# A one-core kernel of two-level attention and a gated feed-forward: when the coarse rows are loaded, where two group sums stand, which queue loads the last v rows, and how the coarse pieces are dealt out to chunks

## The chip, the cores and the metric

The program runs on one core of one Trainium2 chip. The metric is the device time of one execution in microseconds (us); the median of three runs of the kernel before is 1115.64 us (1114.74 to 1118.12). TensorE (PE) multiplies and transposes, VectorE (DVE) and ScalarE (ACT) do the elementwise work, GpSimd (POOL) some of it, and SyncE (SP) only starts transfers. ACT and POOL start transfers too. Every engine works its own list in order: an instruction that waits holds up all that stand behind it on the same engine.

## The reference

Inputs are q, k, v of 8 batches, 8 heads, 576 positions and 64 columns, and three weights of a gated feed-forward.

```python
q_d = q.reshape(B, H, Sd, factor, D).mean(axis=3)      # factor 4; k_d, v_d alike
out_d = sm_attn(q_d, k_d, v_d)
out_up = np.repeat(out_d, factor, axis=2)
mask = np.abs(pos[:, None] - pos[None, :]) < factor
out_local = softmax(where(mask, scale * q @ k^T, -1e9)) @ v
x = (out_up + out_local), heads side by side            # 4608 tokens x 512
xn = x / sqrt(mean(x * x) + 1e-6) * rms_g
out = (silu(xn @ w_gate) * (xn @ w_val)) @ w_out         # 512 -> 1536 -> 512
```

## The kernel before

**Chunks.** The 4608 tokens are worked in 18 chunks of 256 (NCH, numbered from 0). Of each chunk the feed-forward (class Forward) runs over 12 slices f of 128 hidden columns: `first` (L1327) is 24 matmuls for gate and value, then come tanh on ACT (L1335), gate and product on DVE (L1338, L1343), a split of the result in two parts (L1349 on ACT, L1352 on DVE or POOL) and, two slices later, `second` (L1363), 6 matmuls into the output. Each product is made of three matmuls, since numbers are kept as a high and a low part.

**Coarse attention.** It is cut into 32 coarse pieces, one for each batch and pair of heads, numbered 0 to 31 (class Coarse): a score (L524), a softmax, a swap (transposes, L564), values (L579), and a store of the result `o_g` to a tensor `up` in DRAM (L596), one such tensor for each pair of batches. A piece needs the sums over groups of four positions of q, k and v: class Sums, one object for each batch and half of its heads, so that two pieces share one. Its tiles qk and vs are loaded by SP (L358, L362), and three more loads each, which add to what is there, are started by POOL (L366); each of the three must wait until the one before has landed. Each tile name has two buffers.

**Rows of the coarse result.** A chunk's attention needs its rows of `up`. Class Attention loads them into `up_t` in `load_up` (four transfers of a chunk, L783), class Dense in its own `load_up` (L1189). All of these are started by ACT.

**The first three chunks** get their local attention as full scores under a mask (class Dense): the values step (L1166) reads v rows that `load_rows` (L1028) and, for the last row of chunk 0, `load_edge` (L1039) put into the four kv buffers. From chunk 3 on the local attention is elementwise on DVE, ACT and POOL (class Attention: L701, L705, L748, L755, L774), with its own k, v and q loads into the same kv buffers (L607).

**Two ways in which the order is set.** The opening (coarse pieces 0 to 7, attention of chunks 0 and 1, the decoding of 36 weight pieces, the feed-forward of chunk 0) is a list: class Plan takes tasks with an engine, a cost, a due time and buffers, plays them through, and writes the instructions in that order. A weight piece is decoded by `last_bits` on POOL (L267), a scaling on ACT (L257), a join on DVE (L274), a high part on ACT (L286, L284) and a low part (L298 on DVE; for w_out L296 on DVE or L294 on POOL, as the plan chooses). Four of the late pieces pass one after another through a single buffer named `raw`. What is written after the list is ordered by the framework's scheduler, which may also put an instruction without a due time far ahead, into gaps of the list. `tc.issue_after(x)` forbids that it stands ahead of x. PE's instructions after the list are tied to each other in this way.

**Chunks 1 on.** While chunk c runs, the attention of chunk c + 1 is made, and coarse pieces are worked at the slices that PIECES names: score at slice f, swap at f + 2, values at f + 3. All of pieces 8 to 15 (the second pair of batches) must be stored before the second half of chunk 4 can load its rows. Group sums are written at slices 0 and 6 of every chunk, or when a piece first asks for them.

Line numbers in prose are those of the profile of this kernel.

## Time and profile before

| what | value |
|---|---|
| median of three runs | 1115.64 us |
| the profiled execution | 1120.63 us |
| its span, first to last instruction | 1118.4 us |
| PE busy, DVE busy, ACT busy, POOL busy | 94%, 79%, 54%, 19% of the span |
| start of the first matmul of the feed-forward, chunks 0, 1, 2, 3, 4, 5 | 94.8, 161.3, 230.0, 300.7, 366.1, 419.6 us |
| chunk to chunk from chunk 5 on | 55.5 us, from chunk 12 on (no coarse pieces left) 50.8 us |

The profile is of one execution. PE is busy nearly all of the span, so what can be won is where it isn't: the time before 94.8 us, the chunks 0 to 3, which take 65 to 71 us in place of 55.5, and nothing after. The clock column of a stretch is the TensorE clock that was granted, as a share of 2.4 GHz; 0.5 is the lower of its two levels.

### The profile page before, as it was taken

How to read it: one execution, taken by the hardware profiler on the slowest of the kernel's cores; microseconds unless marked ns; L12 is line 12 of the kernel's file. 1: busy time of each engine (PE TensorE's matmuls, PEld its weight loads, DVE VectorE, ACT ScalarE, POOL GpSimd, SP SyncE). 2: the span in 40 equal slices, each digit the busy share in tenths (PEclk: the TensorE clock that was granted, in tenths of full speed). 3: DMA queues.
4: the chain of work that ended last, by engine and by line, in shares of the span. 5: the costliest groups of instructions: out<-in, count | busy, mean ns of one | idle time of the engine just before them, and what ended most of it. 6: DMA issues, size and time to landing. Idle time of an engine off the chain costs nothing.

```text
span 1118.4 us, 23630 instructions
## 1 busy us (share of the span) xinstructions
PE 1054.7 (94%) x8804; PEld 964.9 (86%) x8804; DVE 888.9 (79%) x1850; ACT 603.2 (54%) x2182; POOL 210.4 (19%) x269
## 2 busy tenths in 40 slices
PE   4886887999998999999999999999999999999998
PEld 3565776889897999999999999999999999999997
DVE  5867962987696989797989797979798989987422
ACT  5556732384454656565655555555647383737222
POOL 2244650032311121212121203010102020101000
PEclk9877998999998999999999999999999999999999
DMA  8676363456453343434354444313131322310000
GB/s 260 197 237 228 132 143 67 107 127 138 93 131 68 108 99 108 99 111 96 111 96 121 89 122 90 106 43 99 47 97 53 102 62 76 88 42 20 1 20 19
DMA packets 72681, 113.26 MB, mean 101 GB/s; under 512 B 25974, under 2 KB 33910, under 8 KB 72566
## 3 DMA queue, kind: packets, MB, share of 16 engines
q1 hardware_dynamic: 46422, 91.66, 27.2%
q0 software_dynamic: 8640, 15.93, 9.3%
q10 hardware_dynamic: 17504, 4.16, 1.7%
q8 instruction: 69, 1.13, 0.4%
q14 instruction: 46, 0.38, 0.1%
HBM read 99.92 MB, written 11.80 MB: 100 GB/s over the span
## 4 chain that ended last, share of the span: by engine, by line
PE 79%; DVE 7%; DMA 6%; ACT 4%; issue 3%; POOL 0%; ACTq 0%; SPq 0%; DVEq 0%; POOLq 0%
PE ps_h L1327 46%; PE ps_o L1363 23%; DMA qk<-in_qk_sum_dram 3%; PE ps_a L579 2%; ACT prod L748 2%; PE ps_a L524 1%; DVE prod L701 1%; PE ps_a L850 1%; PE ps_a L564 1%; DMA wv<-in_qk_sum_dram 1%; ACT a_g L555 1%; DMA up<-o_g 1%; PE ps_a L1143 1%; DMA q_t<-in_q_band_dram 1%; DVE sc L705 1%
## 5 line engine op out<-in xcount | busy, mean ns | idle before, releaser
L1363 PE MATMUL ps_o<-wo,hs 128*128 128x512 f32 x1296 | 339.2, 400 | 5.1 <-DVE hs L1352 3.3
L1327 PE MATMUL ps_h<-xh,wg 128*128 128x256 f32 x1728 | 317.6, 280 | 0.0
L1327 PE MATMUL ps_h<-xh,wv 128*128 128x256 f32 x1728 | 312.0, 277 | 0.0
L1327 PEld LDWEIGHTS ps_h<-xh,wg 128*128 128x128 f32 x1728 | 266.8, 190 | 8.1 <-issue 2.7
L1363 PEld LDWEIGHTS ps_o<-wo,hs 128*128 128x128 f32 x1296 | 231.2, 190 | 46.1 <-DVE hs L1352 4.1
L1327 PEld LDWEIGHTS ps_h<-xh,wv 128*128 128x128 f32 x1728 | 264.4, 188 | 2.8 <-issue 0.4
L748 ACT ACTIVATE prod<-kv,sc 128x64 f32<-128x64 f32 x960 | 246.5, 407 | 24.7 <-DMA up<-o_g 10.3
L1327 PE MATMUL ps_h<-xl,wg 128*128 128x256 f32 x864 | 244.4, 283 | 6.2 <-DVE sil L1343 3.8
L1327 PE MATMUL ps_h<-xl,wv 128*128 128x256 f32 x864 | 240.3, 278 | 4.4 <-DVE sil L1338 4.4
L1335 ACT ACTIVATE sil<-ps_h 128x256 f32<-128x256 f32 x216 | 81.7, 379 | 223.5 <-PE ps_h L1327 212.2
L1327 PEld LDWEIGHTS ps_h<-xl,wg 128*128 128x128 f32 x864 | 163.5, 189 | 14.3 <-DVE sil L1343 5.7
L1327 PEld LDWEIGHTS ps_h<-xl,wv 128*128 128x128 f32 x864 | 162.9, 189 | 7.5 <-DVE sil L1338 6.0
L1349 ACT ACTIVATE hs<-sil 128x256 fp32r<-128x256 f32 x216 | 89.4, 414 | 145.1 <-DVE sil L1343 119.5
L755 POOL TENSOR_TENSOR prod<-sc,kv 128x256 f32<-128x256 f32 x120 | 90.3, 790 | 407.0 <-DVE sc L739 202.7
L774 DVE TENSOR_REDUCE x_t<-prod 128x128 f32<-128x896 f32 x120 | 127.9, 1076 | 34.2 <-PE ps_a L850 26.3
L1338 DVE SCALAR_TENSOR_TENSOR sil<-sil,ps_h 128x256 f32<-128x256 f32 x216 | 89.0, 413 | 70.9 <-ACT sil L1335 67.0
L701 DVE TENSOR_TENSOR prod<-q_t,kv 128x896 f32<-128x896 f32 x120 | 129.6, 1082 | 5.4 <-DMA kv<-in_k_pad_dram 4.6
L705 DVE TENSOR_REDUCE sc<-prod 128x14 f32<-128x896 f32 x120 | 128.8, 1074 | 0.0
L1352 DVE TENSOR_TENSOR hs<-sil,hs 128x256 fp32r<-128x256 f32 x208 | 98.7, 476 | 32.6 <-ACT hs L1349 32.4
L1343 DVE SCALAR_TENSOR_TENSOR sil<-sil,ps_h 128x256 f32<-128x256 f32 x216 | 89.7, 416 | 2.8 <-PE ps_h L1327 1.3
L366 POOL DMA_DIRECT2D qk<-in_qk_sum_dram x36 | 32.7, 909 | 237.7 <-DMA qk<-in_qk_sum_dram 163.2
L755 DVE TENSOR_TENSOR prod<-sc,kv 128x128 f32<-128x128 f32 x120 | 51.4, 453 | 0.8
(182 smaller groups left out, 943.9 us busy)
## 6 DMA issues: line engine op xcount, KB each, us to landing
kv<-in_k_pad_dram SPq DMA_DIRECT2D x60, 320.0 KB
kv<-in_v_pad_dram SPq DMA_DIRECT2D x60, 320.0 KB
qk<-in_qk_sum_dram POOLq DMA_DIRECT2D x36, 288.0 KB, 4.9
q_t<-in_q_band_dram SPq DMA_DIRECT2D x60, 128.0 KB
out_dram<-o_sb SPq DMA_DIRECT2D x30, 256.0 KB
vs<-in_v_sum_dram POOLq DMA_DIRECT2D x36, 144.0 KB, 3.4
qk<-in_qk_sum_dram SPq DMA_DIRECT2D x12, 288.0 KB
wo<-in_qk_sum_dram SPq DMA_DIRECT2D x2, 1152.0 KB
```

What stands on the lines that cost most here:

```text
L701: nc.vector.tensor_tensor(out=pr, in0=bcast(q[:, s0:s0 + 2], 2, NO), in1=window(k, s0), op=ALU.mult)
L705: nc.vector.tensor_reduce(out=self.sc[:, j, par, s0:s0 + 2], in_=self.pr[i], axis=AX.X, op=ALU.add,)
L748: nc.scalar.activation(out=self.pr[i][:, o, s], in_=self.v[j, par][:, s0 + s + o], func=AF.Copy, scale=p[:, s, o:o + 1],)
L755: (nc.vector if engine == "DVE" else nc.gpsimd).tensor_tensor(out=self.pr[i][:, a:b], in0=bcast(p[:, :, a:b].rearrange("p s o -> p o s"), ...
L774: nc.vector.tensor_reduce(out=self.x[j][:, s0:s0 + 2, par], in_=pr.rearrange("p o s d -> p s d o"), axis=AX.X, op=ALU.add,)
L1327: last = nc.tensor.matmul(out=self.p[f][:, t], lhsT=wi(f)[:, 0, k], rhs=xi[:, k], start=(n == 0), stop=(n == 3 * KT - 1),).ins
L1335: nc.scalar.activation(out=self.sil[f], in_=self.p[f][:, 0], func=AF.Tanh, scale=0.5)
L1338: nc.vector.scalar_tensor_tensor(out=self.sil[f], in0=self.sil[f], scalar=1.0, in1=self.p[f][:, 0], op0=ALU.add, op1=ALU.mult,)
L1343: nc.vector.scalar_tensor_tensor(out=self.sil[f], in0=self.sil[f], scalar=0.5, in1=self.p[f][:, 1], op0=ALU.mult, op1=ALU.mult,)
L1349: nc.scalar.activation(out=self.hs[f][:, 0], in_=self.sil[f], func=AF.Copy)
L1352: (nc.gpsimd if engine == "POOL" else nc.vector).tensor_tensor(out=self.hs[f][:, 1], in0=self.sil[f], in1=self.hs[f][:, 0], op=ALU.subtract,)
L1363: last = nc.tensor.matmul(out=self.o[j], lhsT=lhs[:, cols], rhs=rhs(f)[:, 0], start=(f == 0 and i == 0), stop=(f == NF - 1 and i == 2),).ins
```

## The change

It has four parts and a fifth that goes with them.

1. `load_up` of Attention and of Dense (after the list) may not be issued ahead of the last copy of chunk 0's output, the list's end (`listed`, `behind`).
2. The two group sums of batch 2 are planned as tasks of the list, due 95 and 103; the two of batch 3 are written at slices 6 and 11 of chunk 1.
3. `load_edge` is started by POOL in place of SP.
4. PIECES: chunk 1 takes four coarse pieces (slices 0, 5, 7, 8), chunk 2 two (0, 3). Chunk 3 keeps two.
5. The v rows of chunk 0 are due earlier (`V_ROWS - 14`, which was `- 9`), so SP starts them ahead of the first weights.

```diff
-PIECES = {1: (0, 5, 8), 2: (0, 3, 6), 3: (0, 2)}
+PIECES = {1: (0, 5, 7, 8), 2: (0, 3), 3: (0, 2)}
+SUMS = {(1, 6): (3, 0), (1, 11): (3, 2)}
...
+    def behind(ins):
+        return tc.issue_after(ins) if ins else nullcontext()
...
-            for t in range(2):
-                nc.scalar.dma_start(out=up[:, t], in_=src[:, :, t, ui])
+            with behind(listed[-1]):
+                for t in range(2):
+                    nc.scalar.dma_start(out=up[:, t], in_=src[:, :, t, ui])
...
-                    t = task("SP", 0.7, lambda a=a: self.load_edge(b, a), V_ROWS - 4.0, [t], uses=[v], dma=0.3)
+                    t = task("POOL", 1.0, lambda a=a: self.load_edge(b, a), 0.0, [t], uses=[v], lag=2.5)
...
-                    V_ROWS - 9.0 + 2 * b + 0.1 * a if at is None else at + 2 * b + a, after, allocs=[v], uses=[v], dma=0.262 * MB,
+                    V_ROWS - 14.0 + 1.0 * b + 0.1 * a if at is None else at + 2 * b + a, after, allocs=[v], uses=[v], dma=0.262 * MB,
...
+            with behind(listed and listed[-1]):
+                for g in range(2):
...
+    for half in range(2):
+        sums[2, half] = Sums(2, half, 125.0 + 8 * half)
...
+    listed.append(opened.copied)
...
-            if f in (0, 6):
+            if (c, f) in SUMS:
+                sums_of(*SUMS[c, f])
+            if f in (0, 6) and c > FIRST:
```

What moves is seen best in the engines' lists. In the changed kernel line numbers are higher by 1 to 7 (L783 is L789, L1207 is L1214, L366 is L367, L267 is L268, L524 is L529, L1327 is L1334, L1363 is L1370).

On ACT, near the end of the opening, where the squares of chunk 0 (L1207) are followed by the weights' scaling. First before, then after:

```order
L286 ACTIVATE wg_0_688<-o_sb,g_sb 128x4x128
L1207 ACTIVATE x_t,ss<-ps_o 128x256
L783 DMA up_t<-up 128x1x64 x3
L1207 ACTIVATE x_t,ss<-ps_o 128x256 x3
L286 ACTIVATE wv_0_754<-o_sb,g_sb 128x4x128
L257 ACTIVATE o_sb<-wg_1_637 128x512
```

```order
L258 ACTIVATE o_sb<-wg_1_624 128x512
L1214 ACTIVATE x_t,ss<-ps_o 128x256 x4
L287 ACTIVATE wg_0_779<-o_sb,g_sb 128x4x128
L258 ACTIVATE o_sb<-wg_1_643 128x512 x2
L258 ACTIVATE o_sb<-wv_1_688 128x512
```

Chunk 3's four loads of coarse rows, which the scheduler had put between the squares, are gone from here; they now stand just after the copies of chunk 0's output.

On POOL, from the last weights to the end of the list. Before, all twelve adding loads of batch 2 stand behind the last weight piece:

```order
L267 TENSOR_SCALAR raw<-raw 128x512
L294 TENSOR_TENSOR wo_1_1734<-o_sb,wo_1_1733 128x512
L1352 TENSOR_TENSOR hs<-sil,hs 128x256 x2
L267 TENSOR_SCALAR raw<-raw 128x512
L366 DMA qk<-in_qk_sum_dram 128x576
L366 DMA vs<-in_v_sum_dram 72x512
L366 DMA qk<-in_qk_sum_dram 128x576
L366 DMA vs<-in_v_sum_dram 72x512
L366 DMA qk<-in_qk_sum_dram 128x576
L1352 TENSOR_TENSOR hs<-sil,hs 128x256
```

After, they stand between the weights, the first of them behind the 28th of the 36 pieces; this is the middle of that stretch:

```order
L367 DMA qk<-in_qk_sum_dram 128x576
L268 TENSOR_SCALAR raw<-raw 128x512
L367 DMA vs<-in_v_sum_dram 72x512
L1359 TENSOR_TENSOR hs<-sil,hs 128x256 x2
L268 TENSOR_SCALAR wo_1_489<-wo_1_489 128x512
L268 TENSOR_SCALAR wo_1_1242<-wo_1_1242 128x512
L367 DMA qk<-in_qk_sum_dram 128x576
L367 DMA vs<-in_v_sum_dram 72x512
L268 TENSOR_SCALAR wo_2_830<-wo_2_830 128x512
L268 TENSOR_SCALAR wo_2_918<-wo_2_918 128x512
L367 DMA qk<-in_qk_sum_dram 128x576
L268 TENSOR_SCALAR raw<-raw 128x512
```

The adding loads no longer end the list; weight pieces that pass through `raw` now stand behind them. POOL does two low parts (L294) and two splits (L1352) fewer in the list, DVE two more of each (L296, L1352); one sum of v (L441) goes from POOL to DVE far ahead of this.

On PE, at the start of chunk 1, the score of piece 8. Before, it stands ahead of the fourth slice; after, ahead of the second (slices are 24 matmuls of L1327 or L1334):

```order
L1327 MATMUL ps_h<-xl,wg_0_688 128x256
L1327 MATMUL ps_h<-xh,wg_0_688 128x256
L1327 MATMUL ps_h<-xh,wg_0_689 128x256
L524 MATMUL ps_a<-qk 72x144 x4
L1143 MATMUL ps_a<-ident_sb,prod 64x64 x16
```

```order
L1370 MATMUL ps_o<-wo_2_1866,hs 128x512 x2
L1370 MATMUL ps_o<-wo_2_1867,hs 128x512
L1334 MATMUL ps_h<-xh,wv_0_845 128x256
L1334 MATMUL ps_h<-xh,wv_0_846 128x256
L529 MATMUL ps_a<-qk 72x144 x4
L1334 MATMUL ps_h<-xl,wg_0_779 128x256
```

The score asks for its sums about two slices earlier; the transposes of chunk 2's scores (L1143, now L1149) follow one slice later.

## Rows read from the trace of the kernel before

**Rows 1.** Windows: us, busy of PE, PEld, DVE, ACT, POOL; clock, DMA share, GB/s.
```profile
161.00:230.00 69.00, 58.11 (x589) 52.88 (x588) 39.29 (x86) 23.97 (x86) 9.01 (x11) 0.93 0.44 96
230.00:300.00 70.00, 68.91 (x544) 62.09 (x544) 54.37 (x124) 39.27 (x153) 17.10 (x21) 1.00 0.58 123
475.00:531.00 56.00, 56.00 (x439) 52.01 (x438) 50.00 (x106) 33.45 (x132) 11.43 (x15) 1.00 0.43 104
```
**Rows 2.** Timeline of ACT near the opening's end: start, us, what, [idle before <-releaser].
```profile
85.06 1.90 ACTq L783 DMA_DIRECT2D up_t<-up  x3
87.01 0.38 ACT L1207 ACTIVATE x_t<-ps_o 128x256 f32<-128x256 f32 x1 [6.20 <-issue]
```
**Rows 3.** Timeline of PE at the same place.
```profile
81.20 0.43 PE L1178 MATMUL ps_o<-o_g,q_t 72*32 72x128 f32 x8
...
91.44 1.94 PE L1249 MATMUL ps_h<-ident_sb,x_t 128*128 128x128 f32 x8 [8.79 <-DVE x_t L1237]
```
**Rows 4.** Timeline of DVE: same place, then two operations of the list's end.
```profile
88.25 0.16 DVE L1216 TENSOR_TENSOR rms<-ss 128x2 f32<-128x2 f32 x1 [3.83 <-ACT x_t L1207]
...
148.25 0.68 DVE L296 TENSOR_TENSOR wo<-o_sb,wo 128x512 fp32r<-128x512 f32 x1
...
157.65 0.41 DVE L1352 TENSOR_TENSOR hs<-sil,hs 128x256 fp32r<-128x256 f32 x1
```
**Rows 5.** The window of 94 to 150 us, columns as in the first group.
```profile
94.00:150.00 56.00, 48.11 (x313) 43.08 (x314) 51.62 (x82) 36.47 (x76) 30.93 (x30) 0.94 0.47 160
```
**Rows 6.** Chain that ended last, at chunk 1's start: start us, us, what.
```profile
154.33 7.03 DMA qk<-in_qk_sum_dram
...
161.70 4.99 DMA qk<-in_qk_sum_dram
...
167.09 9.36 DMA qk<-in_qk_sum_dram
```
**Rows 7.** Timeline of PE in chunk 1's first slices.
```profile
176.59 1.24 PE L524 MATMUL ps_a<-qk 64*72 64x144 f32 x8 [7.26 <-DMA qk<-in_qk_sum_dram]
177.75 1.97 PE L1143 MATMUL ps_a<-ident_sb,prod 128*64 128x64 f32 x32
...
180.04 0.63 PE L1327 MATMUL ps_h<-xh,wg 128*128 128x256 f32 x2
...
183.14 0.39 PE L1327 MATMUL ps_h<-xh,wg 128*128 128x256 f32 x2
...
184.03 1.15 PE L1143 MATMUL ps_a<-ident_sb,prod 128*64 128x64 f32 x32
```
**Rows 8.** The window of 170 to 180 us, columns as in the first group.
```profile
170.00:180.00 10.00, 3.41 (x41) 2.96 (x42) 1.32 (x4) 0.87 (x5) 0.00 (x0) 0.60 0.43 94
```
**Rows 9.** Timeline of POOL: an early gap, and its last split of chunk 0.
```profile
51.05 1.30 POOL L267 TENSOR_SCALAR wg<-wg 128x512 uint32<-128x512 uint16 x1 [10.89 <-DMA wg<-in_w_gate_dram]
...
158.08 0.90 POOL L366 DMA_DIRECT2D qk<-in_qk_sum_dram  x1 [1.33 <-DMA qk<-in_qk_sum_dram]
158.65 1.08 POOL L1352 TENSOR_TENSOR hs<-sil,hs 128x256 fp32r<-128x256 f32 x1
```
**Rows 10.** Timeline of PE: who waits for that split.
```profile
159.79 1.66 PE L1363 MATMUL ps_o<-wo,hs 128*128 128x512 f32 x6 [1.74 <-POOL hs L1352]
```
**Rows 11.** DMA issues of 100 to 180 us: count, KB each, median us to landing.
```profile
qk<-in_qk_sum_dram POOLq DMA_DIRECT2D x6, 288.0 KB, 6.3
```
**Rows 12.** Timeline of SP: the four edge loads, a fetch into the buffer raw, its next.
```profile
47.81 2.31 SPq L1039 DMA_DIRECT2D kv<-in_v_sum_dram  x4
...
116.18 0.33 SPq L253 DMA_DIRECT2D raw<-in_w_gate_dram  x1
...
128.62 0.33 SPq L253 DMA_DIRECT2D raw<-in_w_val_dram  x1
```
**Rows 13.** Chain that ended last, end of chunk 3.
```profile
337.17 6.12 DMA up<-o_g
```
**Rows 14.** Timeline of ACT at that place.
```profile
344.65 0.38 ACT L1335 ACTIVATE sil<-ps_h 128x256 f32<-128x256 f32 x1 [4.84 <-PE ps_h L1327]
```

More of the change, by code (lines that the diff above doesn't have):

```diff
@@ L443, in add_v @@
             )
-    loose = []
+    loose, listed = [], []
+    def behind(ins):
+        return tc.issue_after(ins) if ins else nullcontext()
     used = {"wg": [], "wv": [], "wo": []}
@@ L1038, in load_edge @@
             at = v_sum.offset + ((b * FAC * HALF + HALF - 1) * 2 + a) * DM
-            nc.sync.dma_start(
+            nc.gpsimd.dma_start(
                 out=t[:, :, 1],
@@ L1187, in load_up @@
             src = up_dram[0].rearrange("b k t (s g) d -> s g (b k t) d", g=UPP)[:, self.u0:self.u0 + 2]
-            for g in range(2):
-                nc.scalar.dma_start(out=self.up[g * 16:(g + 1) * 16].rearrange("p (h d) -> p h d", d=D), in_=src[:, g])
+            with behind(listed and listed[-1]):
+                for g in range(2):
+                    nc.scalar.dma_start(out=self.up[g * 16:(g + 1) * 16].rearrange("p (h d) -> p h d", d=D), in_=src[:, g])
         def add_rows(self):
@@ L1370, in copy @@
             self.o_sb[j] = ffn.tile([P, DM], FP32, name="o_sb", bufs=W_BUFS)
-            nc.scalar.copy(out=self.o_sb[j], in_=self.o[j])
+            self.copied = nc.scalar.copy(out=self.o_sb[j], in_=self.o[j]).ins
         def store(self, j):
@@ L1487, in attn_moe_kernel @@
         decode(n)
+    for half in range(2):
+        sums[2, half] = Sums(2, half, 125.0 + 8 * half)
     for c in range(FIRST):
-        Forward(atts[c]).plan(
+        opened = Forward(atts[c])
+        opened.plan(
             first_weights if c == 0 else lambda f: [],
@@ L1497, in attn_moe_kernel @@
     loose.append(True)
-    def behind(ins):
-        return tc.issue_after(ins) if ins else nullcontext()
+    listed.append(opened.copied)
     att, late = atts[FIRST], []
```

## The prediction

> **What bounds the kernel now.** I read first the windows of a chunk each. From chunk 5 on PE is busy without a gap and a chunk takes 55.5 us (the window from 475 us) [rows 1]; there nothing can be won by moving loads. Chunk 1 takes 68.7 us with 58.1 of 69 us busy at a mean clock of 0.93, chunk 2 70.7 us with PE busy 68.9 of 70 [rows 1]: it works off what chunk 1 left behind. So PE is the bound from 230 us on, and a microsecond that PE gets back ahead of 230 us is one off the end, unless something else becomes late. Then I looked in the timelines for what PE waits for before that. Two places stand out.
>
> The first is the end of the opening. ACT has done one of the four squares of chunk 0, then stands 6.20 us in three transfers that load coarse rows [rows 2]: they wait for the store of piece 7. The squares, the root on DVE and PE's transposes all come behind that, and PE idles 8.79 us [rows 3].
>
> The second is chunk 1's first score. Its sums are not ready: three rounds of adding loads follow each other in the chain, 7.03, 4.99 and 9.36 us [rows 6], and PE waits 7.26 us for the last [rows 7], with the clock falling to a mean of 0.60 in that stretch [rows 8].
>
> **Part 1, coarse rows behind the list's end.** Removed: the four transfers between the squares. The tensor that the other three squares read was finished when PE's last add ended, 81.20 + 0.43 = 81.63 us [rows 3]; they began at 87.01 [rows 2]. So x of chunk 0 is ready 5.3 us earlier. The transposes, 1.94 us at 91.44 [rows 3], come behind an idle PE; with a shorter gap they may save another 0.9 (at the higher level the 32 smaller ones of rows 7 took 1.15 us where they took 1.97 behind a gap, so about half is lost): 6.2 at most. But chunk 0's feed-forward then waits for its weights: DVE is busy 51.6 of the 56 us up to 150 us [rows 5], decoding. What DVE gets back is the 3.83 us that it stood idle for those squares [rows 4], and that is my value, **-3.8**; the ends are 0 (weights set the pace throughout) and -6.2. Added: the transfers in chunk 1 or later, on ACT, at 0.63 us each (three took 1.90) [rows 2], 2.5 us for four; ACT has 24 of 69 us busy there [rows 1]. Their source was stored some 70 us before, so they wait for nothing, and who reads them comes a chunk later. Cost 0; without that cover, 2.5 us on the tanh behind them.
>
> **Part 2, sums of batch 2 in the list.** The wait of PE before the score goes: **-7.3** [rows 7]. The clock that it cost goes too: the score, the first transposes and a slice's first matmuls ran at the lower level. Transposes took 1.97 against 1.15 us later, which is 0.8; the score, of 1.24 us, loses 0.5 by the same ratio; a pair of L1327 took 0.63 at 180.04 and 0.39 at 183.14 [rows 7], so from the end of the transposes (179.7) to about 182.3 us, 2.6 us lose 1.0. Together **-2.3**. What is late next there: the score stands a slice or so behind chunk 1's first matmul in either case, and the transposes of chunk 2's scores need shares that DVE has made long before. From chunk 1's values on, the order on PE, SP and DVE is nearly what it was, so the rest of the chunk (k loads after kv is free, the scores of chunk 3 on DVE, the norm of chunk 2 between them) shifts as a whole.
>
> A smaller piece: POOL's last split of chunk 0 stood behind an adding load that had itself waited 1.33 us for a landing [rows 9], and PE waited 1.74 us for the split [rows 10]. I take **-1.0**, between 0 and -1.7.
>
> Added in the list: twelve adding loads on POOL at 0.90 us each [rows 9], 10.8 us, less two L294 and two L1352 that move to DVE. POOL is busy 30.9 of 56 us [rows 5], so the issue time fits; behind these loads are queued the bits of the last eight weight pieces and the low parts of the splits, for which DVE, then PE, wait. A round lands in 6.3 us (median) [rows 11] and three come one after another for each tile, but between two rounds of a tile POOL has four to eight other instructions. I take 0 for the landing waits and keep up to 3 us for the range. DVE takes over two L296 at 0.68 and two L1352 at 0.41 [rows 4]: **+2.2**, all on the path while DVE is the bound, 0 if not.
>
> **Part 3, edges by POOL.** SP loses four issues, 2.31 us [rows 12], ahead of weights; POOL gains four. At the price of an adding load, 0.90 [rows 9], that is 3.6 us, in a gap in which POOL waited 10.89 us for a weight [rows 9]. What is queued behind on POOL are the bits of the first weights. SP now starts the v rows ahead of these weights, some 5 us later for the first two, and DVE has coarse work to do meanwhile. 0; between -2 and +2. The Trainium skill, DMA: Bandwidth & Descriptors, section SWDGE vs HWDGE vs iDMA, speaks against this part: it gives plain transfers to SP and ACT, since POOL computes its descriptors in software. No row shows a plain transfer by POOL; the rows of an adding one (0.90 against SP's 0.58) point the same way, and by them the part would cost 1.3 us if the gap did not hide it.
>
> **Part 4, four pieces in chunk 1, two in chunk 2.** Pieces and matmuls are the same in number up to the start of chunk 3, and PE is full there [rows 1], so it gains nothing and loses nothing by the order. DVE and ACT have room in chunk 1 (39.3 and 24.0 of 69). 0; between -2 and +2. The last store of piece 15 and its reader on ACT, where a tanh waits 4.84 us behind a load of rows [rows 13, 14], stand in chunk 3 as before: nothing is won there, though it looks like the first place.
>
> **The sum.** -3.8 - 7.3 - 2.3 - 1.0 + 2.2 = -12.2 us. The profiled execution took 1120.63, which would become 1108.4. It is 5.0 us above the median of the runs, 1115.64; the difference is put on the median: **1103.4 us**.
>
> **Rivals.**
> (a) The weights set the pace of the opening. Then nothing of part 1 is won, the 2.2 stays, and POOL's rounds cost the last weights 3 us: -7.3 - 2.3 - 1.0 + 5.2 = -5.4, 1110. For it: DVE at 92% up to 150 us [rows 5]. Against: DVE itself idled for ACT just before.
> (b) More than the sum: all of 6.2, the 1.7, no cost on DVE, and 2 us each from parts 3 and 4: -21.5, 1094 at most; its middle is 1097. It needs DVE not to be the bound, against rows 5.
> (c) The change doesn't do what it says: the score of piece 8 finds its sums in time, but chunk 2 can start no earlier, since its x hangs on DVE's 16 large operations for chunk 3, and DVE is caught behind a later k load. Then only part 1 and the clock remain, less the 2.2: between -3.9 and 0, 1114. For it: DVE was the reason for chunk 1's second half. Against: the k loads follow the values step of chunk 2 and shift with it.
> (d) Slower: POOL's rounds hold up the decoding. The buffer raw passes four pieces one by one, a turn took 12.4 us (116.18 to 128.62) [rows 12], and three of them now stand behind rounds of adding loads. If each of the three waits a whole round of 6.3 us [rows 11], chunk 0 ends 18.9 us later, and -12.2 becomes +6.7: 1122. It decides from a landing wait of 4.1 us a turn on; POOL's other work between the rounds speaks against it. In the Trainium skill, the same page, section Anatomy of one DMA, SWDGE path, a transfer by POOL takes 2.0 us and its bytes at 436 GB/s, an estimate of 2.7 us for 288 KB. By it three waits make 8.1 us, and (d) ends at -4.1, or 1111.5. The row on landing here says more than twice that.
>
> **How the numbers follow.** Forecast 0.56, (a) 0.17, (b) 0.07, (c) 0.10, (d) 0.10. The forecast's own range, from its unknown ends, is 1098 to 1109. For 8 in 10 the range takes in (a) and the upper part of (b): 1096 to 1113. A difference of 0.3% (3.3 us) is about what a measurement of this kernel can tell from none. Faster by more than that are the forecast, (b) and nearly all of (a): 0.79; within it (c) and a little of (a): 0.11; slower (d): 0.10.
>
> **What would show it.** Right: four squares in a row on ACT near 82 us and the first matmul of the feed-forward near 89 to 91 us; chunk 1 starting near 157 to 159 us; no wait for a sum ahead of the first score, and a clock of 1.0 through chunk 1's first half; chunk 1 shorter by about 10 us, chunks 3 on unchanged, the wait of ACT at the end of chunk 3 still there. Wrong: POOL idle on qk landings with weight pieces behind it, and chunk 0 longer than 70 us (d); chunk 0 starting early and ending where it did (a); PE in chunk 1 waiting for DVE for as long as it did for the sums (c).

## The result, and the profile after the change

The changed kernel takes 1091.6 us (median of 4 runs, 1090.25 to 1092.73); the kernel before, run beside it, 1116.88. The ratio is 0.9772 (95% interval 0.9745 to 0.9799): 25.3 us faster, twice the forecast 12.2, and outside the range. The same kernel, measured again (after_again, below), took 1089.77 us, ratio 0.9749 (0.9713 to 0.9785). The profiled executions differ by 30.0 us of span (1118.4 and 1088.4), since that of before (1120.63) lies 3.8 us above the median of the runs beside the changed kernel, and that of the changed kernel (1090.25) 1.4 below its own.

Where the time went is read from the first matmul of each chunk's feed-forward. The table gives the start of that matmul in chunk 0 and then the lengths of the chunks, for the two profiled executions and for those of the experiments, which are told further down; from chunk 4 on all agree within 0.4 us a chunk.

| kernel | first matmul | chunk 0 | chunk 1 | chunk 2 | chunk 3 |
|---|---|---|---|---|---|
| before | 94.8 | 66.5 | 68.7 | 70.7 | 65.4 |
| after | 82.8 | 62.8 | 60.1 | 71.7 | 58.3 |
| after_again | 83.1 | 62.6 | 59.4 | 69.9 | 58.4 |
| part1_alone | 86.1 | 68.4 | 72.1 | 71.0 | 60.0 |
| part2_alone | 88.7 | 65.9 | 60.0 | 70.9 | 63.6 |
| part35_alone | 86.7 | 65.8 | 72.4 | 71.0 | 67.1 |
| part4_alone | 91.1 | 67.4 | 67.5 | 73.5 | 58.3 |
| all_but_1 | 85.1 | 62.7 | 60.1 | 70.3 | 58.1 |
| all_but_2 | 83.8 | 65.2 | 74.0 | 72.5 | 63.6 |
| all_but_35 | 90.2 | 66.5 | 60.7 | 69.8 | 58.2 |
| all_but_3 | 85.3 | 65.6 | 61.1 | 72.5 | 58.2 |
| all_but_5 | 90.8 | 67.1 | 60.7 | 70.2 | 58.2 |
| all_but_4 | 83.0 | 64.5 | 59.9 | 71.1 | 63.1 |
| before_16more | 87.0 | 69.1 | 69.0 | 70.7 | 66.5 |
| before_8more | 89.3 | 69.1 | 64.6 | 70.5 | 65.9 |
| after_16more | 84.5 | 62.7 | 59.1 | 69.8 | 58.7 |
| before_mean_first | 89.9 | 68.5 | 66.6 | 71.1 | 63.0 |
| after_earlier | 84.7 | 62.1 | 63.4 | 75.1 | 58.2 |

Four places gained: the opening 12.0, chunk 0 3.7, chunk 1 8.6, chunk 3 7.1 us; chunk 2 lost 1.0. Only chunk 1 is the size that was forecast.

The windows of the changed kernel, one for each of chunks 1, 2, 3 and 5, and then one of chunk 0 (us, busy of PE, PEld, DVE, ACT, POOL; clock, DMA share, GB/s):

```profile
146.00:206.00 60.00, 55.66 (x588) 50.51 (x588) 39.74 (x86) 24.72 (x88) 3.71 (x5) 1.00 0.34 86
206.00:277.00 71.00, 68.83 (x535) 62.80 (x535) 53.95 (x123) 38.98 (x153) 20.17 (x25) 0.98 0.60 126
277.00:336.00 59.00, 59.00 (x454) 53.90 (x453) 50.31 (x109) 33.50 (x132) 11.19 (x14) 1.00 0.43 99
445.00:501.00 56.00, 56.00 (x440) 52.04 (x439) 50.30 (x107) 33.38 (x132) 10.98 (x16) 1.00 0.43 104
...
83.00:146.00 63.00, 55.95 (x374) 49.90 (x375) 57.44 (x102) 41.76 (x85) 39.80 (x41) 0.98 0.75 197
```

Against [rows 1], chunk 1 has a clock of 1.00 in place of 0.93, and in chunk 3 PE is busy for all of 59 us. Chunk 2 still has 2.2 us of idle PE. Against [rows 5], DVE is as full in chunk 0 (57.4 of 63 us), and POOL is fuller, but the DMA share is 0.75 in place of 0.47.

The squares of the changed kernel on ACT, and PE at the same place (start, us, what, idle before and its releaser):

```profile
71.88 0.41 ACT L1214 ACTIVATE x_t<-ps_o 128x256 f32<-128x256 f32 x1
...
72.94 0.43 ACT L1214 ACTIVATE x_t<-ps_o 128x256 f32<-128x256 f32 x1
```
```profile
71.49 0.42 PE L1184 MATMUL ps_o<-o_g,q_t 72*32 72x128 f32 x8 [0.29 <-DVE o_g L598]
...
79.46 1.94 PE L1256 MATMUL ps_h<-ident_sb,x_t 128*128 128x128 f32 x8 [6.51 <-DVE x_t L1244]
82.82 0.58 PE L1334 MATMUL ps_h<-xl,wg 128*128 128x256 f32 x1 [1.42 <-DVE xl L1264]
```

The four squares stand in a row, as part 1 says, and PE's idle time before the transposes is 6.51 in place of 8.79 us [rows 3]. But the last add, which no step of the prediction touched, ends near 71.9 in place of 81.6 us. The opening had become shorter ahead of the place that I looked at.

The score of piece 8 on PE in the changed kernel, and the window around it:

```profile
149.81 0.71 PE L529 MATMUL ps_a<-qk 64*72 64x144 f32 x8
```
```profile
145.00:155.00 10.00, 10.00 (x102) 9.11 (x101) 3.31 (x11) 3.89 (x15) 0.00 (x0) 1.00 0.25 68
```

It waits for nothing, takes 0.71 in place of 1.24 us [rows 7], and the clock is 1.00 in place of 0.60 [rows 8].

### The profile page after: what moved, and what is told of

It reads as the page before. It is cut to its first block, busy times and chain, and to the rows that moved or that the text cites. A ratio compares the mean times of both kernels' runs of the same rounds, so it can differ in the third digit from the quotient of the medians.

```text
span 1088.4 us, 23630 instructions
## 1 busy us (share of the span) xinstructions
PE 1042.2 (96%) x8804; PEld 956.6 (88%) x8804; DVE 889.0 (82%) x1855; ACT 602.3 (55%) x2182; POOL 207.1 (19%) x268
## 4 chain that ended last, share of the span: by engine, by line
PE 85%; DVE 7%; ACT 3%; DMA 2%; issue 2%; POOL 0%; SPq 0%; ACTq 0%; DVEq 0%; POOLq 0%
PE ps_h L1334 51%; PE ps_o L1370 26%; PE ps_a L584 2%; PE ps_a L529 1%; DVE o_sb L275 1%; PE ps_a L856 1%; PE ps_a L569 1%; DMA wv<-in_qk_sum_dram 1%; ACT prod L753 1%; ACT a_g L560 1%; DVE prod L706 1%; DMA qk<-in_qk_sum_dram 1%; DMA q_t<-in_q_band_dram 0%; PE ps_h L1101 0%; PE ps_a L1149 0%
## 5 line engine op out<-in xcount | busy, mean ns | idle before, releaser
L1370 PE MATMUL ps_o<-wo,hs 128*128 128x512 f32 x1296 | 335.8, 397 | 2.0 <-DVE hs L1359 2.0
L1334 PE MATMUL ps_h<-xh,wg 128*128 128x256 f32 x1728 | 317.2, 279 | 0.6 <-DVE wg L299 0.6
L1334 PE MATMUL ps_h<-xh,wv 128*128 128x256 f32 x1728 | 312.2, 278 | 0.0
L1334 PEld LDWEIGHTS ps_h<-xh,wg 128*128 128x128 f32 x1728 | 266.2, 189 | 9.2 <-issue 3.1
L1334 PEld LDWEIGHTS ps_h<-xh,wv 128*128 128x128 f32 x1728 | 264.7, 188 | 3.2 <-issue 0.6
L1370 PEld LDWEIGHTS ps_o<-wo,hs 128*128 128x128 f32 x1296 | 229.0, 188 | 40.7 <-DVE hs L1359 2.4
L1334 PE MATMUL ps_h<-xl,wg 128*128 128x256 f32 x864 | 244.0, 282 | 7.3 <-DVE sil L1350 5.7
L1334 PE MATMUL ps_h<-xl,wv 128*128 128x256 f32 x864 | 240.3, 278 | 4.3 <-DVE sil L1345 4.3
L1334 PEld LDWEIGHTS ps_h<-xl,wg 128*128 128x128 f32 x864 | 163.2, 189 | 15.1 <-DVE sil L1350 7.2
L1334 PEld LDWEIGHTS ps_h<-xl,wv 128*128 128x128 f32 x864 | 162.9, 188 | 7.5 <-DVE sil L1345 6.2
L1345 DVE SCALAR_TENSOR_TENSOR sil<-sil,ps_h 128x256 f32<-128x256 f32 x216 | 88.9, 411 | 58.7 <-ACT sil L1342 56.1
L367 POOL DMA_DIRECT2D qk<-in_qk_sum_dram x36 | 32.9, 913 | 233.5 <-DMA qk<-in_qk_sum_dram 195.5
```

What stands on the lines that cost most here:

```text
L1334: last = nc.tensor.matmul(out=self.p[f][:, t], lhsT=wi(f)[:, 0, k], rhs=xi[:, k], start=(n == 0), stop=(n == 3 * KT - 1),).ins
L1345: nc.vector.scalar_tensor_tensor(out=self.sil[f], in0=self.sil[f], scalar=1.0, in1=self.p[f][:, 0], op0=ALU.add, op1=ALU.mult,)
L1370: last = nc.tensor.matmul(out=self.o[j], lhsT=lhs[:, cols], rhs=rhs(f)[:, 0], start=(f == 0 and i == 0), stop=(f == NF - 1 and i == 2),).ins
```

## The experiments

Four kernels with one part alone (3 and 5 count as one), and four with one part undone, come first. The edits, in the changed kernel, that undo a part:

```diff
 part 1 undone
-    listed.append(opened.copied)
+    listed.append(None)
 part 2 undone
-    for half in range(2):
-        sums[2, half] = Sums(2, half, 125.0 + 8 * half)
...
-            if (c, f) in SUMS:
-                sums_of(*SUMS[c, f])
-            if f in (0, 6) and c > FIRST:
+            if f in (0, 6):
 part 3 undone
-            nc.gpsimd.dma_start(
+            nc.sync.dma_start(
...
-                    t = task("POOL", 1.0, lambda a=a: self.load_edge(b, a), 0.0, [t], uses=[v], lag=2.5)
+                    t = task("SP", 0.7, lambda a=a: self.load_edge(b, a), V_ROWS - 4.0, [t], uses=[v], dma=0.3)
 part 5 undone
-V_ROWS - 14.0 + 1.0 * b + 0.1 * a
+V_ROWS - 9.0 + 2 * b + 0.1 * a
 part 4 undone
-PIECES = {1: (0, 5, 7, 8), 2: (0, 3), 3: (0, 2)}
+PIECES = {1: (0, 5, 8), 2: (0, 3, 6), 3: (0, 2)}
```

A part alone is the kernel before with that part only, so the other edits are undone. The kernel before was measured anew beside each of the four groups of kernels, with medians of 1116.3, 1114.0, 1118.9 and 1117.1 us, in the order of this text. Those of the changed kernel are 1091.6 and 1089.8. What a part costs when undone is given as a difference of medians; for all_but_1, 2, 35 and 4, beside which the kernel before was fastest, the ratios give 1.6 to 4.4 us more.

### Each part alone

> The kernel before with part 1 alone: the coarse rows' loads may not be issued ahead of the last copy of chunk 0's output. Theory A (the 12 us that the opening lost come from two places, this one and the v rows with their edges): the last add of the coarse result stays at 81.2 us on PE, the four squares stand in a row right behind it, the first matmul of the feed-forward falls from 94.8 to 88.5 to 89.5 us, and the whole gets 4 to 6.5 us shorter, to 1110 to 1113. Theory B (these loads are the cause of all 12): first matmul near 83 us, whole near 1104. The recorded prediction said -3.8. If the weights set the pace of chunk 0, the first matmul comes earlier and chunk 1 still starts at 161 us: 0.

Measured: 1115.99 us, ratio 1.0000 (0.9972 to 1.0028). The opening is shorter, and chunk 1 takes it back: 72.1 us. PE in chunk 1 of this kernel:

```profile
171.76 1.24 PE L529 MATMUL ps_a<-qk 64*72 64x144 f32 x8 [9.18 <-DMA qk<-in_qk_sum_dram]
```

The score waits 9.18 us for its sums, against 7.26 before [rows 7]. So neither theory: an earlier opening runs into the sums.

> The kernel before with part 2 alone: the group sums of batch 2 in the list, those of batch 3 at slices 6 and 11 of chunk 1. Theory A: chunk 1 shrinks from 68.7 to about 60 us, chunk 0 stays within 1.5 us of its 66.5, chunks 2 and 3 stay: the whole gets 7 to 10 us shorter, 1106 to 1110. Theory B (chunk 0's 3.7 us that the change won belong to the sums, since POOL's last split no longer stands behind an adding load): chunk 0 near 63, the whole 11 to 13 us shorter, 1103 to 1105. The recorded prediction: -8.4. If the adding loads held up decoding, chunk 0 would be over 70.

Measured: 1106.95 us, ratio 0.9897 (0.9858 to 0.9936), 9.4 us less. Chunk 1 is 60.0 us, chunk 0 65.9. Theory A, and the recorded -8.4.

> The kernel before with parts 3 and 5 alone: edges by POOL, v rows of chunk 0 ahead of the first weights. Theory A (the opening's other half): chunk 0's values on PE begin near 49.5 in place of 55.8 us, the pause of 1.97 us at 60.6 us and the lower clock behind it are gone, the last add of the coarse result ends 6 to 9 us earlier, the first matmul of the feed-forward comes 5 to 8 us earlier, and the whole is 4 to 8 us shorter: 1108 to 1112. Theory B (the recorded prediction): 0, within 2. Theory C: the opening is earlier, but the loads of coarse rows on ACT still wait for their stores, and chunk 0 takes the gain back, since the weights now come later: -2 to 0.

Measured: 1114.95 us, ratio 0.9981 (0.9957 to 1.0005). The first matmul comes at 86.7 us, near the time that theory A wants, and again chunk 1 (72.4 us, a wait of 7.49 us for the sums) and chunk 3 (67.1) take it back. The whole, 1.4 us less, is what theories B and C gave, for the reason of neither: the opening did become shorter, and chunk 0 (65.8) did not take it back.

> The kernel before with part 4 alone: four coarse pieces in chunk 1, two in chunk 2. Theory A (chunk 3's 7.1 us belong to this part: with it a whole slice of the feed-forward stands between the mean's matmul and the turn at the end of chunk 3, where the trace of before has none): opening and chunk 0 as before, chunk 1 and 2 together within 2 us, chunk 3 near 58 to 60 in place of 65.4, whole 5 to 8 us shorter, 1108 to 1111. Theory B (the recorded prediction): 0, chunk 3 still 65. Theory C: chunk 1, which waits for its sums with one more piece to come, gets longer by what chunk 3 wins: 0.

Measured: 1112.58 us, ratio 0.9964 (0.9939 to 0.9990), 3.7 us less. Chunk 3 falls to 58.3 us, as in the changed kernel. Theory A holds for the place, not for the whole; 2.8 us go back in chunk 2 (73.5).

The four add up to 14.8 us (0.3, 9.4, 1.4, 3.7), and all together give 25.3.

### Each part undone

> The changed kernel with part 1 undone: the coarse rows' loads may again stand between the squares of chunk 0. Theory I (the parts help each other: what the opening wins is kept only where the sums are ready at chunk 1's first score): the squares are split again by loads that wait for a store, the first matmul of the feed-forward comes 4 to 7 us later than the 82.8 of the changed kernel, chunk 0 wins back at most 2, and the whole is 3 to 6 us longer than 1091.6: 1094.5 to 1098. Theory II (each part adds what it gives alone, and part 1 alone gave nothing): 1091 to 1093.

Measured: 1091.72 us, ratio 0.9804 (0.9767 to 0.9841): not told apart from the changed kernel. By the medians it costs 0 to 2 us, by the ratios 3.6 to 6, and the intervals of the ratios overlap. ACT and then PE in this kernel:

```profile
75.34 1.90 ACTq L789 DMA_DIRECT2D up_t<-up  x3
77.29 0.39 ACT L1214 ACTIVATE x_t<-ps_o 128x256 f32<-128x256 f32 x1 [5.69 <-issue]
```
```profile
81.72 1.94 PE L1256 MATMUL ps_h<-ident_sb,x_t 128*128 128x128 f32 x8 [9.37 <-DVE x_t L1244]
```

ACT stands 5.69 us between the squares again, and PE idles 9.37 us. Yet the first matmul is only 2.0 to 2.3 us later, where theory I had 4 to 7. The root on DVE in the changed kernel tells why; beside it, POOL:

```profile
73.89 1.25 DVE L1223 TENSOR_TENSOR rms<-ss 128x2 f32<-128x2 f32 x1
...
76.10 0.47 DVE L1236 SCALAR_TENSOR_TENSOR newton<-rinv 128x2 f32<-128x2 f32 x1
...
78.24 0.16 DVE L1236 SCALAR_TENSOR_TENSOR newton<-rinv 128x2 f32<-128x2 f32 x1
```
```profile
71.50 3.61 POOL L295 TENSOR_TENSOR wo<-o_sb,wo 128x512 fp32r<-128x512 f32 x1 [1.54 <-ACT wo L285]
75.20 2.09 POOL L268 TENSOR_SCALAR wv<-wv 128x512 uint32<-128x512 uint16 x3
77.37 0.64 POOL L268 TENSOR_SCALAR wg<-wg 128x512 uint32<-128x512 uint16 x1
```

The operations on 128x2 took 0.16 or 0.17 us before ([rows 4] has the first), and the chain from the first of them to the norm 2.56 us (88.25 to 90.81). After, every other one takes 0.47 to 1.25 us while POOL is busy, up to 78.01 us, and 0.16 from then on; the chain takes 4.94 us (73.89 to 78.83). In all_but_1 the chain begins at 78.53 us, when POOL has stopped (its last operation there ends at 78.15), and takes 2.56 us again. So 2.4 us of what part 1 won went into a root that now stands beside POOL's work.

> The changed kernel with part 2 undone: no sums of batch 2 in the list. Theory I (the score of piece 8 takes back what the opening wins): the first matmul comes near 83 to 84 us as in the changed kernel, chunk 1 is longer than the 60.1 us of the changed kernel by 11 to 14, more than the 8.6 that part 2 gave alone, and the whole is near 1106 to 1111. Theory II (the parts add up): the whole is 9.4 us longer than 1091.6, 1100 to 1102.

Measured: 1112.01 us, ratio 0.9969 (0.9937 to 1.0001): 20 to 22 us over the changed kernel, where part 2 alone gave 9.4. Theory I, and more than it expected. PE at the score, and the window of chunk 1, in this kernel:

```profile
167.85 1.24 PE L529 MATMUL ps_a<-qk 64*72 64x144 f32 x8 [8.49 <-DMA qk<-in_qk_sum_dram]
```
```profile
149.00:223.00 74.00, 60.57 (x589) 55.11 (x587) 40.47 (x87) 25.56 (x92) 10.63 (x13) 0.88 0.47 101
```

The wait is 8.49 us, the clock of chunk 1 0.88 on average. It is the one part without which the others give next to nothing.

> The changed kernel with parts 3 and 5 undone: edges by SP, v rows of chunk 0 after the first weights. Theory I: the pause of PE near 61 us and the lower clock behind it are there again in the profiled execution, the first matmul of the feed-forward comes 4 to 7 us later than 82.8, and all of it reaches the end: 1095 to 1099, with a spread of the runs like that of the kernel before (over 8 us). Theory II (the parts add up, and these gave 1.4 alone): 1092 to 1094. The recorded prediction, which put them at 0: 1091 to 1092.

Measured: 1102.25 us, ratio 0.9900 (0.9856 to 0.9944): 10.7 to 12.5 us over the changed kernel, more than either theory. The first matmul comes at 90.2 us and chunk 0 takes 66.5. The runs spread by 4.0 us, not by 8.

> The changed kernel with part 4 undone: three pieces in chunk 1, three in chunk 2. Theory I (chunk 3's 7.1 us are part 4's): chunks 0 and 1 as in the changed kernel, chunk 2 about 1 us shorter, chunk 3 at 63 to 66 in place of 58.3, whole 4 to 6.5 us longer than 1091.6: 1095.5 to 1098. Rival (chunk 3 also shrank by 5.4 with part 1 alone, so the other parts suffice): chunk 3 near 58 to 60 all the same, whole 1090 to 1092.5.

Measured: 1095.53 us, ratio 0.9836 (0.9796 to 0.9876): 3.9 to 5.8 us over. Chunk 3 takes 63.1 us. Theory I.

### Edges or rows, and the pause of PE

> The changed kernel once more, beside the next three. Both theories: 1088 to 1093, a spread of its runs under 4 us, the first matmul of the feed-forward near 83 us, chunks 0 to 3 near 62.8, 60.1, 71.7 and 58.3.

Measured: 1089.77 us (1087.86 to 1093.05), ratio 0.9749 (0.9713 to 0.9785). As expected, but for 5.2 us of spread.

> The changed kernel with part 3 undone: edges by SP, v rows still ahead of the first weights. Theory I (what counts is that the v rows stand ahead of the weights, so chunk 0's values begin near 49.5): within 3 us of the changed kernel. Theory II (SP's four edge loads, which wait until the rows have landed, hold the weights behind them; POOL takes them off that queue): values begin near 55, PE pauses near 62 us, first matmul near 90, whole 7 to 11 us longer, as with both undone.

Measured: 1098.23 us, ratio 0.9817 (0.9789 to 0.9846), 8.5 us over after_again. The first matmul comes at 85.3 us, chunk 0 takes 65.6. The whole and the pause (below) are as theory II says; the first matmul, which it put near 90 us, is not.

> The changed kernel with part 5 undone: v rows of chunk 0 due as before, edges by POOL. Theory I (the v rows' place counts): values begin near 55, PE pauses near 62 us, first matmul near 90, whole 7 to 11 us longer. Theory II (the edges' queue counts): within 3 us of the changed kernel.

Measured: 1099.37 us, ratio 0.9826 (0.9790 to 0.9861), 9.6 us over. The first matmul comes at 90.8 us: theory I. So both are wanted: without either most of the gain is lost.

Where the gain lies is seen at the adds of the coarse result on PE, six from 40 us on. Here are the third and the fourth of them, first before, then after:

```profile
56.91 0.43 PE L1178 MATMUL ps_o<-o_g,q_t 72*32 72x128 f32 x8
...
68.96 0.66 PE L1178 MATMUL ps_o<-o_g,q_t 72*32 72x128 f32 x8
```
```profile
56.87 0.42 PE L1184 MATMUL ps_o<-o_g,q_t 72*32 72x128 f32 x8
...
63.03 0.43 PE L1184 MATMUL ps_o<-o_g,q_t 72*32 72x128 f32 x8 [0.30 <-DVE o_g L598]
```

The third comes at 56.9 us in both; the fourth is 5.9 us earlier after, and the sixth 9.7 (81.20 in [rows 3], 71.49 above). Up to 60 us the transfers move as much in both, 6.5 MB from 30 us on, though in another order. The windows from 60 to 70 us of before, after and all_but_5, columns as above:

```profile
60.00:70.00 10.00, 8.03 (x127) 6.82 (x116) 4.69 (x11) 4.46 (x15) 0.64 (x1) 0.64 0.87 265
```
```profile
60.00:70.00 10.00, 9.51 (x156) 7.83 (x152) 8.77 (x21) 9.25 (x31) 4.16 (x5) 1.00 1.03 336
```
```profile
60.00:70.00 10.00, 6.90 (x125) 6.26 (x125) 4.89 (x12) 3.68 (x13) 1.29 (x2) 0.66 0.86 254
```

DVE and ACT are half idle before and in all_but_5, at a clock of 0.64 and 0.66, and nearly full after. (In part2_alone, part4_alone and all_but_3 the clock of this window is 1.00 and DVE busy 7.3 to 8.1 us.) The weights follow, since on SP they stand behind the stores of `o_g`: on POOL, the bits of 8 pieces have been begun by 60 us in both, and by 80 us those of 13 before and of 18 after. The last of the 36, on POOL in before and after:

```profile
151.84 0.67 POOL L267 TENSOR_SCALAR raw<-raw 128x512 uint32<-128x512 uint16 x1 [2.23 <-DMA raw<-in_w_out_dram]
```
```profile
138.59 0.65 POOL L268 TENSOR_SCALAR raw<-raw 128x512 uint32<-128x512 uint16 x1 [1.87 <-DMA raw<-in_w_out_dram]
```

Decoding ends 13 us earlier, and with it chunk 0: in all 18 profiles chunk 0 ends 3.9 to 7.0 us behind that last piece where part 2 is in, and 7.4 to 11.5 us where it is not.

What the kernels without parts 3 and 5 have in common near 61 us is a pause of PE in the middle of 64 like matmuls, with no releaser. This is PE of the kernel before:

```profile
59.63 0.99 PE L1166 MATMUL ps_o<-kv,x_t 64*32 64x64 f32 x56
62.59 0.32 PE L1166 MATMUL ps_o<-kv,x_t 64*32 64x64 f32 x8 [1.97 <-issue]
```

The pause stands behind the 56th in before (1.97 us), part1_alone (0.50), part2_alone (1.04), part4_alone (1.79), before_mean_first (1.15), all_but_35 (2.86), all_but_5 (3.10) and all_but_3 (1.15), and in none that has both parts. The longer it is, the fewer weight pieces are begun by 80 us: 13 to 15 with 2 to 3 us, 15 or 16 with 1.0 to 1.8, 17 or 18 with 0.5 or none. Three kernels shift PE's instructions by repeating transposes that write the same values again:

```diff
 before_16more and after_16more; before_8more has (0, 1, 2, 3, 3)
-            for x in range(4):
+            for x in (0, 1, 2, 3, 2, 3) if (self.c, par) == (0, 1) else range(4):
```

> The kernel before with the last eight transposes of the first flips of chunk 0 issued twice (the same values written again), which puts 16 matmul records and 16 weight loads more on PE ahead of the second half of chunk 0's values. Theory P (PE's pause near 61 us is a wait for its own code, which arrives in pieces of a fixed number of instructions): the pause moves by as many instructions, to behind the 40th of the 64 matmuls, from behind the 56th. Theory Q (the pause is a wait for data of that matmul, such as the edge rows): it stays behind the 56th. Time: within 1% of the kernel before under both.

Measured: 1113.81 us, ratio 0.9940 (0.9912 to 0.9967). No pause is seen there at all, so neither sentence came true. The sixth add on PE in this kernel:

```profile
76.53 0.43 PE L1178 MATMUL ps_o<-o_g,q_t 72*32 72x128 f32 x8
```

It comes 4.7 us earlier than before, half of the 9.7, and the first matmul of the feed-forward at 87.0 us. Useless work made the kernel about 5 us faster (3.7 to 9.8 by the interval). What is left of the 9.7 goes with the order: in the changed kernel the second values of chunk 0 stand at 55.84 us, ahead of the third add, and before at 59.63, between it and the fourth. All profiles say the same. The sixth add comes at 70.9 to 73.1 us where both parts are in; at 74.2 in all_but_3; in the other nine at 76.5 without the pause and at 76.8 to 82.1 with it. So the order is worth some 4 us there, and what goes with the pause up to 5 more.

> The kernel before with the last four transposes of the first flips of chunk 0's second half issued twice, 16 records more on PE. Theory P: no pause behind the 56th of the 64 matmuls of chunk 0's second values; it stands behind the 48th, or is not seen, as with 32 records more. Theory Q: it stays behind the 56th. Where the pause is gone, the first matmul of the feed-forward comes near 87 us in place of 91 to 95, and the whole is about 0.5% shorter; where it is there, within 0.3%.

Measured: 1115.10 us, ratio 0.9989 (0.9966 to 1.0012). PE of this kernel:

```profile
61.39 0.88 PE L1166 MATMUL ps_o<-kv,x_t 64*32 64x64 f32 x48
63.23 0.43 PE L1166 MATMUL ps_o<-kv,x_t 64*32 64x64 f32 x16 [0.97 <-issue]
```

Behind the 48th, and the whole within 0.3%, as theory P says.

> The changed kernel with the last eight transposes of chunk 0's second flip issued twice, 32 records more on PE from about 42 us on. Theory P (PE waits for code at fixed instruction numbers): the pause of about 1 us behind the 5th of 8 matmuls of a score at 46 us goes from there; it stands 32 records earlier, inside the 16 matmuls of the coarse values before it, or is not seen. Theory Q (a wait for data): it stays behind the 5th matmul of that score. Time: within 3 us of 1089.8 under both.

Measured: 1091.19 us, ratio 0.9762 (0.9732 to 0.9791). PE of this kernel:

```profile
44.21 0.74 PE L584 MATMUL ps_a<-vs,a_g 72*72 72x64 f32 x9
45.83 0.61 PE L584 MATMUL ps_a<-vs,a_g 72*72 72x64 f32 x7 [0.88 <-issue]
46.27 0.55 PE L543 MATMUL ps_h<-q_t 128*128 128x224 bf16 x4
46.75 0.71 PE L529 MATMUL ps_h<-qk 64*72 64x144 f32 x8
```

The score's eight matmuls run through, and the pause stands in the coarse values before it. Theory P in both kernels: the pause belongs to a place in PE's program, not to the data of a matmul.

### The end of chunk 3, and the border of chunks 1 and 2

> The kernel before with one move: the last slice of chunk 3 may not be issued ahead of the mean's matmul of chunk 4, so that this slice stands between the mean and the turn, as in the changed kernel. Theory M (that slice covers the root on DVE): chunk 3 falls from 65.4 to 58 to 61 us, all else stays, the whole is 4 to 7 us shorter, 1108 to 1113. Theory N (the wait of ACT behind piece 15's store sets the end of chunk 3, and PE only waits elsewhere): chunk 3 stays over 64, the whole within 2 us.

```diff
-            last = fwd.emit(f)
+            with behind(mean if (c, f) == (3, 11) else None):
+                last = fwd.emit(f)
             for step in before.get(f, ()):
                 with behind(last):
                     last = step()
+                if f == 8:
+                    mean = last
```

Measured: 1116.83 us, ratio 1.0007 (0.9983 to 1.0031). PE of this kernel:

```profile
345.86 0.39 PE L806 MATMUL ps_a<-ss,same_sb 128*128 128x8 f32 x2 [3.97 <-ACT up_t L799]
```

(The mean is PE's small matmul over the squares of the next chunk, L806 or L812; a root on DVE, a norm and the turn, PE's transposes of the result, follow it.) Theory M falls: PE now waits at the mean for ACT's squares. Theory N is the better one, though chunk 3 (63.0) is under its 64. Counted from the start of chunk 3, the mean stands at 46.6 or 46.7 us in after, after_again, part4_alone, all_but_1 and all_but_35 (chunk 58.1 to 58.4 us), at 48.0 in part1_alone (60.0), 49.8 in before_mean_first (63.0), 50.3 in all_but_4 (63.1), 50.9 in part2_alone (63.6), 51.2 in before (65.4), 52.0 in all_but_2 (63.6) and 53.0 in part35_alone (67.1). The chunk ends 11.5 to 14.2 us behind the mean, and the mean follows the last coarse piece's store and its readers on ACT. These are they in the changed kernel:

```profile
312.45 0.30 ACTq L601 DMA_DIRECT2D up<-o_g  x1
...
315.75 1.20 ACTq L789 DMA_DIRECT2D up_t<-up  x2
317.06 0.38 ACT L1342 ACTIVATE sil<-ps_h 128x256 f32<-128x256 f32 x1 [3.27 <-issue]
...
321.48 0.29 ACT L805 ACTIVATE up_t<-x_t 128x128 f32<-128x128 f32 x1
```

From the store to its reader it takes 3.3 us, where the chain of before had 6.12 [rows 13], and the store stands 1.4 us earlier in the chunk (35.1 in place of 36.5). Part 4 alone does not settle the place: part1_alone, without it, has a wait of 3.9 us and a chunk 3 of 60.0, and all_but_2, with it, a store 40.4 us into the chunk and a chunk 3 of 63.6. The transfers between store and reader, in before and in after:

```profile
DMA packets 806, 0.94 MB, mean 147 GB/s; under 512 B 372, under 2 KB 500, under 8 KB 805
```
```profile
DMA packets 483, 0.41 MB, mean 121 GB/s; under 512 B 328, under 2 KB 328, under 8 KB 483
```

Before, SP starts a load of k or v and one of q (448 KB) at 336.71 and 337.35 us, just when the store goes out; after, those two start at 308.46 and 309.09, 3 to 4 us ahead of it. Whether the store is slow for their company stays open: where they go out together it took 3.9 us (part1_alone), 4.2 (before_mean_first) and 4.3 (all_but_4), and 5.9 to 7.2 in five others; where they go ahead of it, 2.7 to 4.5.

> The changed kernel with the second piece of chunk 1 at slice 3 in place of 5 and the first sums of batch 3 written at slice 4 in place of 6. Theory S (the loss left at the border of chunks 1 and 2 is POOL, which stands in waits of 4.03 and 2.99 us for adding loads ahead of its part of the attention): PE's waits of 2.12, 1.12 and 2.17 us there go, chunks 1 and 2 together fall from 131.8 to 126 to 129, the whole to 1084 to 1088. Theory D (DVE is full there, 9 to 10 of 10 us, and sets the pace): within 2 us of 1089.8.

```diff
-PIECES = {1: (0, 5, 7, 8), 2: (0, 3), 3: (0, 2)}
-SUMS = {(1, 6): (3, 0), (1, 11): (3, 2)}
+PIECES = {1: (0, 3, 7, 8), 2: (0, 3), 3: (0, 2)}
+SUMS = {(1, 4): (3, 0), (1, 11): (3, 2)}
```

Measured: 1099.33 us, ratio 0.9835 (0.9807 to 0.9862), 7.7 to 9.6 us slower than the changed kernel; both theories missed. POOL and then PE in this kernel:

```profile
201.87 0.95 POOL L367 DMA_DIRECT2D qk<-in_qk_sum_dram  x1 [4.84 <-PE ps_a L569]
207.00 0.87 POOL L367 DMA_DIRECT2D qk<-in_qk_sum_dram  x1 [4.18 <-DMA qk<-in_qk_sum_dram]
211.75 0.86 POOL L367 DMA_DIRECT2D qk<-in_qk_sum_dram  x1 [3.88 <-DMA qk<-in_qk_sum_dram]
212.31 0.99 POOL L760 TENSOR_TENSOR prod<-sc,kv 128x256 f32<-128x256 f32 x1
```
```profile
221.15 0.58 PE L1334 MATMUL ps_h<-xl,wg 128*128 128x256 f32 x1 [7.96 <-DVE sil L1350]
```

The sums did not come earlier. All three rounds now stand ahead of POOL's part of the attention, which begins when the last is issued, and PE waits 7.96 us at the end of that. The mechanism of theory S is there; this edit made it worse.

## Why the prediction was wrong, step by step

**Part 2 was right.** -8.4 was forecast for the wait, its clock and POOL's split, less DVE's extra work; chunk 1 lost 8.6 to 9.3 us, and alone the part gives 9.4. What the step lacked is that it decides over the rest: without it the score waits 7.5 to 9.2 us for sums wherever the opening ends earlier, so gains ahead of it are not kept (part1_alone, part35_alone, all_but_2). The prediction wrote its terms as a sum; they are not one.

**Part 1 was probably sized too high.** -3.8 was the value, 0 to -6.2 the ends. The stall went as described, but undone it moves the first matmul by only 2.0 to 2.3 us, since the root on DVE slowed from 2.56 to 4.94 us beside POOL. Of the whole it costs 0 to 2 us by the medians; the ratios (3.6 to 6) don't exclude the -3.8. The step "what DVE gets back is the 3.83 us" took the durations of DVE's small operations over to a place where POOL works.

**Parts 3 and 5 were put at 0; they are the largest error.** Undone together they cost 10.7 to 12.5 us. The step of the prediction that failed is the one that priced them by SP's and POOL's issue times alone and asked which work hides these: "0; between -2 and +2". What the parts move is on PE: with rows and edges there early, both values of chunk 0 leave the coarse chain's way, the pause at 61 us is gone, and the chain that ends the opening is 9.7 us shorter. The pause stood in the trace of before, as did the clock of 0.64 from 60 to 70 us; the rows of PE that I took from that trace begin at 81.20 us [rows 3], where the idle time was largest, and I took the chain ahead of them as given. The Trainium skill, DMA: Bandwidth & Descriptors, section SWDGE vs HWDGE vs iDMA, spoke against plain transfers by POOL; here the part paid: with the edges back on SP the kernel is 8.5 us slower. POOL took 0.57 to 0.83 us to issue one of them, where the prediction took the 0.90 of an adding load.

**The 2.2 us for DVE and chunk 0.** DVE stayed as full as it was, but chunk 0 is 3.7 us shorter, as the weights come earlier. No run shows the 2.2 by itself. all_but_35 (66.5) and all_but_2 (65.2) show that it takes both parts 2 and 3 with 5.

**Part 4 was put at 0; it gives 4 to 6.** The step that failed is "stand in chunk 3 as before: nothing is won there". I compared where piece 15's store and its reader stand in the program, and not when they come beside other transfers and ACT's other work. Part 4 makes the store 1.4 us earlier in its chunk and its wait 2 to 3 us shorter, and the mean, which PE's end of chunk 3 hangs on, comes 4.5 us earlier. What makes the wait shorter stays open.

**The rivals.** (d) did not come: in chunk 0 POOL waited 3.0 us in all for landings of adding loads (2.51 and 0.44), and a round of qk landed in 5.0 us. (a) and (c) did not come either. (b) lay nearest with 1094 to 1097, but for its reasons only in part: of the two parts that it gave 2 us each, one brought 4 to 6 and the other over 10.

**The profiled execution.** Its 5 us over the median were put down as such, and the difference was taken from the median. That held: 30.0 us between the profiles, 25.3 between the medians. But its opening, the place that I read most closely, was the slowest that was seen: the first matmul at 94.8 us, and at 87.0 to 91.1 in the four other profiles that have the same opening but for repeated transposes (part4_alone, before_16more, before_8more, before_mean_first).

## What to carry to other kernels

The largest idle time on the bounding engine is where a chain ends; follow that chain back to its start before a move along it is priced at nothing. Try each part of a change both alone and undone: where one wait stands behind several gains, the parts are worth little alone and much together. A wait that "stays in its place" is to be checked for its time against what else is transferred then, not for its place in the list.

## What the runs showed that was not expected

PE's pauses without a releaser lie at fixed places of its program. Counted over all of PE's records in the trace (weight loads, matmuls and the few semaphore rows), those between 25 and 70 us stand at record 449, 705, 961, 1217 or 1729 in all of the 18 profiles, always 256 or a multiple of it apart; repeating transposes moved the matmul that waits, not the number. The transfers have a queue of the kind "instruction", and this is the window of the pause in the kernel before:

```profile
DMA packets 286, 0.66 MB, mean 277 GB/s; under 512 B 133, under 2 KB 133, under 8 KB 285
...
q1 hardware_dynamic: 285, 0.65, 103.0%
q8 instruction: 1, 0.02, 2.8%
```

One packet of that queue lies among 285 of the loads, which keep the engines at 103%. The reading that fits is that PE's code comes in such pieces through the same DMA engines and is late when they are full. The times of these packets, 16 KB each, bear the first half out. In the kernel before, PE stops at 60.62 us; the packet goes from 60.25 to 61.31; PE goes on at 62.59. In all 55 such pauses of the 18 profiles PE goes on 1.2 to 1.6 us after a packet has landed. In before_16more it landed at 60.22 us and PE came to record 1729 only at 61.90, so there was no pause. For the second half, here are the windows from PE's passing of record 1473, 256 records ahead, to the start of the packet, in before and in after:

```profile
56.10:60.25 4.15, 4.04 (x132) 2.92 (x125) 3.35 (x9) 3.62 (x13) 2.93 (x3) 1.00 1.00 291
```
```profile
52.53:52.74 0.21, 0.21 (x5) 0.11 (x2) 0.21 (x2) 0.21 (x2) 0.17 (x1) 1.00 0.09 39
```

The packet starts 4.15 us behind that place with the DMA engines full, and 0.21 us behind it with a DMA share of 0.09. In the nine kernels that pause at record 1729 it starts 2.5 to 4.9 us behind, with a share of 0.91 to 1.03. Of the nine that don't, it starts 1.3 and 1.8 us behind in before_16more and after_16more, also with full engines, and no later than 1.0 us behind in the seven others, with a share of at most a third. So a late packet goes with full DMA engines in every profile; that the transfers make it late was not tried by itself. A shift of 32 records took this pause away, and 0.6% of the time with it. The pauses were 0.4 to 3.1 us long, and the clock behind them did not always fall in the same stretch: 0.64 from 60 to 70 us in before, 1.00 in all_but_35 with a longer pause.
